# A gated convolution and MLP mix on one core: the work as a graph on a deadline list schedule, exchanges through DRAM in large transfers, a 512-column second DFT step, gate sums on TensorE

## The chip, the cores and the metric

The kernel runs on one core of a Trainium2 chip. The metric is the device time of one launch in microseconds (us), as the median of several executions. Some executions of a kernel are slower as a whole, at a lower granted TensorE clock (the slow state); all times quoted are of runs in the fast state. The engines are called TensorE (PE in profile lines, PEld for its weight loads), VectorE (DVE), ScalarE (ACT), GpSimd (POOL) and SyncE (SP), which issues all DMA transfers here. SBUF is the memory on the chip from which the engines work, PSUM the one that takes the results of matmuls; copying a result from PSUM to SBUF is called its eviction. A slab is one of the 16 groups of 128 positions.

## The reference, cut to what matters

Two branches read the same input `q` of 2048 positions by 640 channels. Branch A is a short shift convolution of `k`, times `v`, then a long convolution along the 2048 positions (by FFT of length 4096), times `q`. Branch B is a mixer and MLP. A sigmoid gate mixes them.

```python
x = A_q
g = sigmoid((x * gate_w).sum(-1, keepdims=True))      # the gate sums
a = _A_ref(x, A_k, A_v, A_shift_k, A_ssm_k, A_ssm_D)  # k shift, kv, rfft * rfft(ssm_k), irfft, q * y
b = _B_ref(x, B_w1, B_w2, B_w3, B_w4)                 # layernorm, w1, gelu, shifts, w2, +x,
                                                      # layernorm, w3 (640->1536), gelu, w4, +
return g * a + (1 - g) * b
```

The FFT is done as matrix products. The 2048 positions lie as 128 partitions by 16. A first step contracts the 128 partitions with DFT tables. Then the 16 residues of each frequency must come to lie in neighbouring partitions: that is the *exchange*. A second step multiplies by small 16-point DFTs, set block by block into a 128x128 matrix. The spectrum of the kernel (H) and of the data (X) are multiplied, and the second step, an exchange and the first step follow backwards (V, inverse).

## The kernel before

The program is written as passes over half of the channels and half of the frequencies, and each engine runs its instructions in program order. The exchange is one transfer from SBUF to SBUF for each of 16 residues, of 80 KB in runs of 640 bytes. W3/W4 come in bursts between passes.

```python
    def exchange(dst, stage, lo):
        nc.sync.dma_start(out=dst, in_=stage.rearrange("(a r) t d -> a r t d", a=8)[:, lo])

    def x_pass(dh, h):
        step1(KV, dh, h, False)                      # first step, into GR (SBUF)
        for kp in range(T1 // 2):
            ps = pst()
            gx = ring.tile([P, 2, DH], BF16, name="gx", bufs=3)
            for j in range(2):
                exchange(gx[:, j, :], GR, 2 * kp + j)
                nc.tensor.matmul(ps[:, j, 0:DH], lhsT=M3[:, 0, :], rhs=gx[:, j, :], start=True, stop=True)
            xs = ring.tile([P, 2, DH], BF16, name="xs")
            nc.scalar.copy(out=xs[:], in_=ps[:, :, 0:DH])
            pq = ring.tile([P, 2, 2, DH], BF16, name="pq", tag="pv", bufs=3)
            nc.vector.tensor_tensor(out=pq[:], in0=xs[:].unsqueeze(2).to_broadcast([P, 2, 2, DH]),
                                    in1=HH[:, 2 * kp:2 * kp + 2], op=ALU.mult)
            pv = pst()
            for j in range(2):
                nc.tensor.matmul(pv[:, j, 0:DH], lhsT=M3[:, 1, :], rhs=pq[:, j, 0, :], start=True, stop=False)
                nc.tensor.matmul(pv[:, j, 0:DH], lhsT=M3[:, 2, :], rhs=pq[:, j, 1, :], start=False, stop=True)
            nc.scalar.copy(out=VR[:, h, 2 * kp:2 * kp + 2, :], in_=pv[:, :, 0:DH])
    ...
    def gate():
        for s in range(T1):
            junk = ring.tile([P, D], BF16, name="junk", tag="xy", bufs=3)
            nc.vector.scalar_tensor_tensor(out=junk[:], in0=QX[:, s, :], scalar=1.0, in1=GW[:], op0=ALU.mult,
                                           op1=ALU.mult, accum_out=Z[:, s:s + 1])
    ...
    x_pass(0, 0)
    h_pass(0, 1)
    w3_chunk(0)
    x_pass(0, 1)
    w4_chunk(0)
    h_pass(1, 0)
    gq_half(0)
    inv(0)
    w3_chunk(1)
    x_pass(1, 0)
    h_pass(1, 1)
    w4_chunk(1)
    w3_chunk(2)
    ...
```

## Time and profile before

| | before |
|---|---|
| time | 528.44 us (528.3 to 528.58, 2 runs) |
| span of the profiled run | 522.9 us |
| TensorE, VectorE, ScalarE busy | 61%, 41%, 30% |
| mean granted TensorE clock | 0.728 |

The page of the profile. The first line below gives the busy time of each engine. The rows under it cut the span in 40 slices: busy tenths, and for PEclk the granted clock in tenths of full speed (9 is 90% or more). The last line is the chain of waits that ended last, by what it spent its time on.

```profile
PE 317.2 (61%) x1597; PEld 159.9 (31%) x1608; DVE 216.5 (41%) x444; ACT 159.0 (30%) x214; POOL 19.7 (4%) x49
...
PE   0196654992146459446945488355488835559797
PEclk9998985896555659755965569556579955558899
DMA  8970206403610250521125510210520241344001
...
DMA gx<-GR 12%; PE ps L451 11%; PE ps L461 10%; DMA vx<-R_70 5%; DVE pq L403 5%; ACT GR L376 4%; PE ps L407 4%; ACT xs L401 4%; DVE bst L220 4%; PE ps L408 3%; SPq L364 3%; DVE R_72 L358 2%; DVE junk L315 2%; DVE R_72 L359 2%; PE ps L302 2%
```

No engine is busy all the time, and the largest entry of the chain is the wait for an exchange. Past the first six slices the clock row follows the busy row: where TensorE is at 5 tenths or less, its clock is mostly 5 or 6.

The timeline of an x pass, VectorE alone (start, duration, what, and in brackets the idle time before and what ended it):

```profile
226.84 0.83 DVE L403 TENSOR_TENSOR pq<-xs,R_71 128x1280 bf16<-128x1280 bf16 x1 [2.63 <-ACT xs L401]
230.30 0.83 DVE L403 TENSOR_TENSOR pq<-xs,R_71 128x1280 bf16<-128x1280 bf16 x1 [2.63 <-ACT xs L401]
233.76 0.82 DVE L403 TENSOR_TENSOR pq<-xs,R_71 128x1280 bf16<-128x1280 bf16 x1 [2.63 <-ACT xs L401]
```

One pair of residues takes 3.46 us, the same each time. In it VectorE works 0.83 us and waits 2.63 us for ScalarE, which waits for TensorE, which has waited for VectorE: the matmuls of the next pair stand behind the products of this one in TensorE's order. TensorE in the same pass, with its wait before the first exchange matmul and then before the products of each pair:

```profile
217.89 0.45 PE L399 MATMUL ps<-gx,M_140 128*128 128x320 bf16 x1 [4.53 <-DMA gx<-GR]
...
224.26 0.42 PE L407 MATMUL ps<-pq,M_140 128*128 128x320 bf16 x1 [1.70 <-DVE pq L403]
...
227.72 0.42 PE L407 MATMUL ps<-pq,M_140 128*128 128x320 bf16 x1 [1.70 <-DVE pq L403]
```

The granted clock was 1.00 up to 214 us, fell to 0.50 from 215 us on, within the wait of 4.53 us, and stayed at 0.50 in the pass (219.5 to 233.5 us), where TensorE is half busy and no gap from 221 us on is longer than 1.70 us.

Busy time of each engine in three stretches (an x pass, an h pass, a W4 burst), with the granted clock. The columns are window, its length, busy us and count of PE, PEld, DVE, ACT, POOL, then clock, DMA share, GB/s:

```profile
142.00:170.00 28.00, 15.16 (x53) 7.21 (x53) 10.31 (x22) 10.27 (x16) 0.45 (x2) 0.50 0.11 24
262.00:283.00 21.00, 8.44 (x25) 1.79 (x24) 0.00 (x0) 9.14 (x15) 0.00 (x0) 0.60 0.41 94
246.24:260.69 14.45, 14.45 (x97) 9.80 (x95) 2.65 (x3) 0.69 (x1) 0.00 (x0) 0.91 0.21 46
```

### The profile page before, as it was taken

To read this page: it belongs to the slowest core of one execution; us is meant where nothing else is said; L and a number is where in the kernel's file an instruction comes from. 1 tells how busy PE (TensorE), PEld (TensorE's weight loads), DVE (VectorE), ACT (ScalarE), POOL (GpSimd) and SP (SyncE) were. 2 spreads that over 40 slices of the span, in tenths; PEclk is the share of its full clock that TensorE was granted. 3 is DMA by queue.
4 is the path that set the end of the run, shared out by engine and by line. 5 is a ranking of instruction groups with operands and counts; after the bars stand their busy time and mean duration, and the time that the engine had idled before them with its cause. 6 is when DMAs were issued, how large, how long until landed. Compare 5 with 4: busy or idle time off the path is not lost.

```text
span 522.9 us, 4484 instructions
## 1 busy us (share of the span) xinstructions
PE 317.2 (61%) x1597; PEld 159.9 (31%) x1608; DVE 216.5 (41%) x444; ACT 159.0 (30%) x214; POOL 19.7 (4%) x49
## 2 busy tenths in 40 slices
PE   0196654992146459446945488355488835559797
PEld 0163320670022124123611143122055312115455
DVE  6988999999841020321201140121014041344402
ACT  0534553005033423533052016335301633100030
POOL 5121000000200000000000000000000000000000
PEclk9998985896555659755965569556579955558899
DMA  8970206403610250521125510210520241344001
GB/s 326 373 269 0 89 14 140 137 8 146 200 42 8 61 128 13 145 52 38 43 59 127 116 26 0 66 36 2 136 64 0 64 104 36 76 101 150 25 1 50
DMA packets 47638, 45.34 MB, mean 87 GB/s; under 512 B 2688, under 2 KB 44545, under 8 KB 47232
## 3 DMA queue, kind: packets, MB, share of 16 engines
q1 hardware_dynamic: 47616, 45.06, 31.0%
q8 instruction: 12, 0.20, 0.2%
q14 instruction: 10, 0.08, 0.0%
HBM read 21.46 MB, written 2.62 MB: 46 GB/s over the span
## 4 chain that ended last, share of the span: by engine, by line
PE 35%; DVE 26%; DMA 18%; ACT 9%; issue 6%; SPq 3%; POOL 1%; ACTq 0%
DMA gx<-GR 12%; PE ps L451 11%; PE ps L461 10%; DMA vx<-R_70 5%; DVE pq L403 5%; ACT GR L376 4%; PE ps L407 4%; ACT xs L401 4%; DVE bst L220 4%; PE ps L408 3%; SPq L364 3%; DVE R_72 L358 2%; DVE junk L315 2%; DVE R_72 L359 2%; PE ps L302 2%
## 5 line engine op out<-in xcount | busy, mean ns | idle before, releaser
L403 DVE TENSOR_TENSOR pq<-xs,R_71 128x1280 bf16<-128x1280 bf16 x32 | 26.4, 824 | 97.2 <-ACT xs L401 97.2
L407 PE MATMUL ps<-pq,M_140 128*128 128x320 bf16 x64 | 28.7, 449 | 56.8 <-DVE pq L403 56.8
L453 ACT ACTIVATE R_78<-ps 128x1024 bf16<-128x1024 f32 x24 | 24.6, 1024 | 120.8 <-PE ps L451 120.8
L451 PE MATMUL ps<-XNT,R_76 128*128 128x512 bf16 x232 | 56.1, 399 | 5.6 <-DVE XNT L247 4.7
L385 PE MATMUL ps<-gx,M_140 128*128 128x320 bf16 x64 | 27.9, 436 | 49.4 <-DMA gx<-GR 48.4
L461 PE MATMUL ps<-R_72,R_78 128*128 128x320 bf16 x384 | 57.7, 314 | 0.0
L464 DVE SCALAR_TENSOR_TENSOR QX<-ps,OMG,QX 128x640 bf16<-128x640 f32 x16 | 14.1, 884 | 81.3 <-PE ps L461 81.3
L376 ACT CAST GR<-ps 128x640 bf16<-128x640 f32 x64 | 39.1, 733 | 20.7 <-PE ps L373 20.7
L461 PEld LDWEIGHTS <-R_78 128*128 128x128 bf16 x384 | 39.3, 102 | 18.6 <-issue 1.0
L409 ACT CAST R_70<-ps 128x640 bf16<-128x640 f32 x32 | 22.1, 692 | 72.1 <-PE ps L408 72.1
L399 PE MATMUL ps<-gx,M_140 128*128 128x320 bf16 x64 | 24.2, 468 | 22.4 <-DMA gx<-GR 22.3
L386 ACT ACTIVATE R_71<-ps 128x640 bf16<-128x640 f32 x32 | 22.5, 704 | 49.4 <-PE ps L385 49.4
L428 PE MATMUL ps<-vx,I_75 128*128 128x320 bf16 x64 | 25.3, 440 | 19.9 <-DMA vx<-R_70 19.4
L451 PEld LDWEIGHTS <-R_76 128*128 128x128 bf16 x240 | 24.5, 103 | 36.2 <-issue 10.1
L431 DVE TENSOR_TENSOR KV<-ps,KV 128x640 bf16<-128x640 f32 x16 | 13.2, 825 | 52.5 <-PE ps L428 52.5
L241 PE MATMUL pt<-IDN,xn 128*128 128x128 bf16 x160 | 15.1, 254 | 29.4 <-DVE xn L236 29.2
L408 PE MATMUL ps<-pq,M_140 128*128 128x320 bf16 x64 | 30.2, 472 | 0.0
L408 PEld LDWEIGHTS <-M_140 128*128 128x128 bf16 x64 | 8.1, 127 | 70.8 <-issue 67.1
L220 DVE BATCH_NORM_STATS2 bst<-QX 128x6 f32<-128x320 bf16 x64 | 27.7, 468 | 4.3 <-DMA QX<-in_A_q_dram 4.3
L264 PE MATMUL ps<-XNT,R_76 128*128 128x512 bf16 x97 | 25.3, 417 | 5.9 <-ACT XNT L245 5.6
L401 ACT CAST xs<-ps 128x640 bf16<-128x640 f32 x32 | 22.3, 696 | 19.5 <-PE ps L399 19.5
L385 PEld LDWEIGHTS <-M_140 128*128 128x128 bf16 x64 | 4.2, 110 | 71.1 <-DMA gx<-GR 71.1
(79 smaller groups left out, 348.9 us busy)
## 6 DMA issues: line engine op xcount, KB each, us to landing
gx<-GR SPq DMA_DIRECT2D x128, 80.0 KB
R_71<-R_71 SPq DMA_DIRECT2D x16, 320.0 KB
vx<-R_70 SPq DMA_DIRECT2D x64, 80.0 KB
R_70<-in_A_k_dram SPq DMA_DIRECT2D x3, 1120.0 KB
QX<-in_A_q_dram SPq DMA_DIRECT2D x4, 640.0 KB
R_71<-in_A_ssm_k_dram SPq DMA_DIRECT2D x5, 512.0 KB
KV<-in_A_v_dram SPq DMA_DIRECT2D x4, 640.0 KB
KV<-in_A_q_dram SPq DMA_DIRECT2D x8, 320.0 KB
```

What stands on the lines that cost most here:

```text
L220: nc.vector.bn_stats(out=st[:, i, j, :], in_=QX[:, s, j * DH:(j + 1) * DH])
L264: nc.tensor.matmul(ps[:, j, :], lhsT=lhsT, rhs=xt[:, k, :], start=(k == 0), stop=(k == DT - 1))
L376: nc.scalar.copy(out=GR[:, 2 * tp:2 * tp + 2, :], in_=ps[:, :, 0:DH])
L385: nc.tensor.matmul(ps[:, j, 0:DH], lhsT=M3[:, 0, :], rhs=gx[:, j, :], start=True, stop=True)
L401: nc.scalar.copy(out=xs[:], in_=ps[:, :, 0:DH])
L403: nc.vector.tensor_tensor(out=pq[:], in0=xs[:].unsqueeze(2).to_broadcast([P, 2, 2, DH]), in1=HH[:, 2 * kp:2 * kp + 2], op=ALU.mult)
L407: nc.tensor.matmul(pv[:, j, 0:DH], lhsT=M3[:, 1, :], rhs=pq[:, j, 0, :], start=True, stop=False)
L408: nc.tensor.matmul(pv[:, j, 0:DH], lhsT=M3[:, 2, :], rhs=pq[:, j, 1, :], start=False, stop=True)
L428: nc.tensor.matmul(ps[:, j, 0:DH], lhsT=I1[:, h, t1, :], rhs=vx[:, j, h, :], start=(h == 0), stop=(h == 1))
L451: nc.tensor.matmul(ps[:, j, :], lhsT=W3[:, k, (f0 + j) * P:(f0 + j + 1) * P], rhs=xt[:, k, :], start=(k == 0), stop=(k == DT - 1))
L453: nc.scalar.activation(out=GTP[:, (3 * c + f0 // 4) % 5, f0 % 4:f0 % 4 + 2, :], in_=ps[:], func=ACT.Gelu_apprx_tanh)
L461: nc.tensor.matmul(ps[:, j, 0:DH], lhsT=GTP[:, (3 * c + f // 4) % 5, f % 4, i * P:(i + 1) * P], rhs=W4[:, f, j * DH:(j + 1) * DH], start=( ...
```

## The change

The intent is to let W3/W4 and the transforms run at the same time, to make exchanges few and large, and to take work off VectorE. Every piece of work becomes a node with a cost on each engine that could do it, dependences, buffers of small rings, and a deadline. A greedy list scheduler, run while the program is built, puts the nodes into one static order for each engine. The text below is cut to the core.

```diff
+class Plan:
+    def add(self, name, alts, fn, deps=(), bufs=(), mode=None, tgt=None, after=0.0, nbytes=0, rate=370.0):
+    ...
+    def schedule(self):            # rank = latest start, from deadlines and successors; greedy by rank
+    ...
-    def exchange(dst, stage, lo):
-        nc.sync.dma_start(out=dst, in_=stage.rearrange("(a r) t d -> a r t d", a=8)[:, lo])
+            wr.append(pl.dma("%sw%d" % (pref, c), lambda e, c=c, sb=sb: nc.sync.dma_start(
+                out=dram.rearrange("h p t d -> p h t d")[:, :, 2 * c:2 * c + 2, :], in_=SG[:, sb.idx]), ...
+    ...
+        def rd(dram, e, xb, h=h, hb=hb):
+            nc.sync.dma_start(out=XIN[:, xb.idx].rearrange("p (m d) -> p m d", m=8),
+                              in_=dram[h].rearrange("p t d -> (p t) d").rearrange("(m q) d -> q m d", q=P)[:, hb:hb + 8, :])
+    ...
-                nc.tensor.matmul(ps[:, j, 0:DH], lhsT=M3[:, 0, :], rhs=gx[:, j, :], start=True, stop=True)
+            for C in range(2):     # the other branch, TILE64, works in 64x64 quarters; it is off
+                nc.tensor.matmul(pt[:, C, :], lhsT=M3[:, m, :], rhs=rhs_fn(None, C), start=start, stop=stop)
+    ...
-            nc.vector.scalar_tensor_tensor(out=junk[:], in0=QX[:, s, :], scalar=1.0, in1=GW[:], op0=ALU.mult,
-                                           op1=ALU.mult, accum_out=Z[:, s:s + 1])
+                        for k in range(DT):
+                            nc.tensor.matmul(ps(pb)[:, 1, i:i + 1], lhsT=XNT[:, xb.idx, k, i * P:(i + 1) * P],
+                                             rhs=GWT[:, k:k + 1], start=(k == 0), stop=(k == DT - 1))
+    ...
+    plan = pl.schedule()
+    with tc.manual_schedule():
+        for n in plan:
+            n.fn(n.eng)
```

The gate sums on TensorE use the normalized rows that are there already for W1, and are turned back into sums of `q` with mean and deviation. The graph also shares evictions between ScalarE and VectorE, takes the statistics of the second layernorm from accumulators, and fuses gate, `q` and eviction in the output stage.

## The prediction

> **What bounds the kernel now.** No engine does. The summary of the profile has TensorE at 61% (317.2 us), VectorE 41% (216.5), ScalarE 30%. The chain of waits is a serial alternation: "DMA gx<-GR" 12%, "DMA vx<-R_70" 5%, its issue on SP 3%, pq 5%, xs 4%, GR eviction 4%. The timeline of an x pass repeats every 3.46 us: ScalarE copy 0.70, VectorE product 0.83, four matmuls, eviction, next pair; TensorE has about 1.5 us of work in it. The stretches of transform passes (75-92, 142-195, 208-246, 262-306, 320-381, 413-475 us: some 230 us) hold TensorE about half busy, and the granted clock there is 0.50-0.60, against 0.9-1.0 in the W3/W4 bursts. That agrees with the Trainium skill, "TensorE: Matmul & The Clock Gate" (Part 1: idle windows put the array at half clock). So serial exchange costs twice: the wait and the slow clock.
>
> **What the change does.** Matmul columns stay the same (about 528 thousand): W1-W4, 132 first-step and 64 inverse matmuls as before; the second step becomes 160 matmuls of 512 columns in place of 256 of 320. In dense bursts the trace shows 0.20-0.24 us per 512 columns (one W3 chunk: 60 in 13.9 us) and 0.135-0.155 per 320 (W4: 96 in 13.0-15.0). 500 x 0.23 + 676 x 0.145 + 272 transposes x 0.07 + gate matmuls 5 = 237 us of TensorE if warm.
> VectorE, by issue spacing (0.73 us for 640 PSUM elements or 1280 bf16): removed are 12 us of gate sums and half of the layernorm statistics; added are half of the evictions (28 of 1024 elements, about 1.13 us; 22 of 640). Sum about 220-225 us. ScalarE stays near 150.
> DMA: 192 exchange issues of 80 KB at 0.6 us each on SP become about 36 large ones, but through DRAM: about 36 MB of exchange and swaps instead of 21, about 60 MB in all; at the 345-370 GB/s of the first load stretch about 170 us, now mostly hidden.
>
> **How much is on the critical path.** Nearly all of the exchange waits, since the list schedule puts W3/W4 work between transform matmuls. What remains serial: all first-step outputs must be written before a read, and all four V writes before the inverse. Stages, estimated from those durations:
> - load, layernorm, W1, H step 1, W2: three engines each about 75-80 us, coupled through four PSUM buffers: about 97;
> - k shift (64 products, 47 us of VectorE) with X step 1 and W3/W4: about 60;
> - second step and products (VectorE about 62): about 75;
> - V write, reads, inverse, 16 fused outputs (VectorE 18 us, DMA 10 MB), stores: about 35;
> - outside the span (528.4 against 522.9): 5.5.
> About 272; with static-order stalls I predict 280 us, 80% range 256 to 322. Faster by over 2%: 0.985; within 2%: 0.01; slower: 0.005.
>
> **What would show each step right.** TensorE over 80% busy, mean clock 0.85-0.95 instead of 0.73; VectorE 75-85% and the co-limit; no exchange in the chain above 5% except around the X read and in the last 35 us; DMA share 60-70%, few packets under 1 KB. The gate sums should vanish from the 62-73 us chain.
>
> **What would make it wrong.** A static order that misjudges DMA latency: one late landing stalls all engines and drops the clock. DRAM turnarounds above 5 us, or 1280-byte rows well under 300 GB/s, would push it towards 320. VectorE evictions slower than estimated add directly in the last three stages. If stages overlap better than assumed, 255.

## The result, and the profile after

| | before | after |
|---|---|---|
| time | 528.44 us | 280.64 us (280.39 to 280.9, 2 runs) |
| ratio of fast runs | 1 | 0.531, 95% interval 0.5295 to 0.5325 |
| span of the profiled run | 522.9 us | 278.6 us |
| TensorE, VectorE, ScalarE busy | 61%, 41%, 30% | 87%, 83%, 52% |
| mean granted clock | 0.728 | 0.983 |

Ratios here and below are the mean time of one kernel's fast runs over that of the other's fast runs of the same rounds, so not quite the ratio of the medians that stand beside them. The experiments ran later, on several chips, each beside the kernel before but not beside the kernel after; the median of the kernel before lay between 526.66 and 529.52 us there. Differences of a few us from the kernel after are therefore good to some 2 us only (an estimate from the intervals of the ratios).

The same lines of the page, after:

```profile
PE 243.2 (87%) x1597; PEld 144.7 (52%) x1597; DVE 230.7 (83%) x424; ACT 144.9 (52%) x177; POOL 26.5 (10%) x59
...
PE   4389989699999999989979899999999799899650
PEclk9999999889999999999999999999999999999995
DMA  7998414029994021294041999852999450589974
...
PE PS L763 13%; PE PS L860 11%; PE PS L775 11%; DMA CJ<-in_A_q_dram 5%; DMA RK<-GHD 4%; PE PS L580 4%; DVE RK L823 4%; DVE RK L827 4%; PE PS L677 3%; DMA RK<-in_A_k_dram 3%; PE PS L731 2%; DVE SX L348 2%; DVE RK L957 2%; DVE W L426 2%; DVE QX L781 1%
```

Between the load phase and the tail TensorE stands at 8 or 9 in nearly all slices, with the clock at 8 or 9 from the first slice to the 39th. The chain is now 47% matmuls and 31% VectorE, and the one exchange at the top of it is 4%. The work itself has hardly changed. That both pages count 1597 matmuls is chance: in the first trace 11 matmul records are missing (it has 1608 weight loads), and the second kernel has 160 matmuls of 512 columns in the second step in place of 256 of 320, and 85 of one column for the gate (1608 - 96 + 85 = 1597). The smaller busy time comes mostly from the second step: with the same number of columns it is 111.0 us busy before and 40.7 after, while W4 is 57.7 and 54.4. The clock is a part of that; how large a part, no run separates.

Five stretches after (same columns): the load phase; W1, the first step of H and part of W2; the rest of W2 and the k shift with the first step of X; the second step; and the tail.

```profile
0.00:24.00 24.00, 14.30 (x111) 12.20 (x112) 19.96 (x44) 11.55 (x11) 9.64 (x32) 1.00 0.92 320
24.00:78.00 54.00, 49.07 (x381) 29.34 (x380) 46.96 (x152) 43.44 (x60) 8.27 (x18) 0.97 0.54 200
78.00:153.00 75.00, 71.72 (x463) 43.62 (x463) 72.92 (x125) 37.02 (x56) 8.58 (x11) 1.00 0.37 130
165.00:225.00 60.00, 57.91 (x326) 30.14 (x325) 49.91 (x49) 37.51 (x38) 0.00 (x0) 1.00 0.78 271
250.00:278.60 28.60, 15.96 (x108) 10.12 (x105) 21.67 (x35) 0.00 (x0) 0.00 (x0) 0.89 0.83 282
```

What is left over lies at the ends. In the first 24 us TensorE works 14.3 us beside loads at about 320 GB/s. In the last 28.6 us it works 16.0, and the chain of the tail tells why:

```profile
250.27 1.74 DVE RK L957 x3
252.01 6.86 DMA CJ<-in_A_q_dram
258.89 1.68 DVE RK L957 x2
...
263.11 4.07 DMA CJ<-in_A_q_dram
...
268.97 3.68 DMA CJ<-in_A_q_dram
```

`CJ<-in_A_q` is the reload of `q` for the output stage: it has two buffers, so a load can start only when a product has given one back, and the chain waits 6.86 + 4.07 + 3.68 = 14.6 us for three of them.

### The profile page after: what moved, and what is told of

Read it like the earlier page. It is cut to its first block, busy times and chain, and to the rows that moved or that the text cites. A ratio compares the mean times of both kernels' runs of the same rounds, so it can differ in the third digit from the quotient of the medians.

```text
span 278.6 us, 4239 instructions
## 1 busy us (share of the span) xinstructions
PE 243.2 (87%) x1597; PEld 144.7 (52%) x1597; DVE 230.7 (83%) x424; ACT 144.9 (52%) x177; POOL 26.5 (10%) x59
## 2 busy tenths in 40 slices
DMA packets 32788, 60.89 MB, mean 219 GB/s; under 512 B 2304, under 2 KB 19457, under 8 KB 32384
## 4 chain that ended last, share of the span: by engine, by line
PE 47%; DVE 31%; DMA 12%; issue 4%; ACT 4%; POOL 0%; SPq 0%; DVEq 0%; ACTq 0%; POOLq 0%
PE PS L763 13%; PE PS L860 11%; PE PS L775 11%; DMA CJ<-in_A_q_dram 5%; DMA RK<-GHD 4%; PE PS L580 4%; DVE RK L823 4%; DVE RK L827 4%; PE PS L677 3%; DMA RK<-in_A_k_dram 3%; PE PS L731 2%; DVE SX L348 2%; DVE RK L957 2%; DVE W L426 2%; DVE QX L781 1%
## 5 line engine op out<-in xcount | busy, mean ns | idle before, releaser
L775 PE MATMUL PS<-W,RG 128*128 128x320 bf16 x384 | 54.4, 299 | 2.9 <-ACT RG L767 1.4
L763 PE MATMUL PS<-XNT,W 128*128 128x512 bf16 x240 | 54.4, 379 | 0.1
L344 ACT CAST SX<-PS 128x640 bf16<-128x640 f32 (+1 forms) x55 | 40.2, 775 | 26.9 <-PE PS L731 22.7
L775 PEld LDWEIGHTS <-RG 128*128 128x128 bf16 x384 | 37.5, 98 | 19.3 <-issue 4.2
L767 ACT ACTIVATE RG<-PS 128x1024 bf16<-128x1024 f32 x24 | 24.6, 1023 | 25.8 <-PE PS L763 25.6
L763 PEld LDWEIGHTS <-W 128*128 128x128 bf16 x240 | 23.5, 98 | 27.8 <-issue 0.7
L348 DVE CAST SX<-PS 128x640 bf16<-128x640 f32 (+1 forms) x29 | 26.1, 914 | 4.4 <-issue 3.3
L781 DVE SCALAR_TENSOR_TENSOR QX<-PS,ZG,QX 128x640 bf16<-128x640 f32 x16 | 14.1, 881 | 17.9 <-PE PS L775 17.9
L677 PE MATMUL PS<-R 128*128 128x320 bf16 x160 | 25.0, 307 | 0.5 <-DVE ZG L606 0.3
L916 DVE TENSOR_TENSOR SX<-SX,R 128x2048 bf16<-128x2048 bf16 x20 | 24.1, 1219 | 0.2
L677 PEld LDWEIGHTS <-R 128*128 128x128 bf16 x160 | 16.0, 101 | 8.1 <-issue 1.3
L580 PEld LDWEIGHTS <-R 128*128 128x128 bf16 x100 | 9.9, 99 | 11.7 <-issue 0.6
```

What stands on the lines that cost most here:

```text
L344: nc.scalar.copy(out=o, in_=i)
L348: nc.vector.tensor_copy(out=o, in_=i)
L580: nc.tensor.matmul(ps(pb)[:, j, :], lhsT=lhsT, rhs=XNT[:, xb.idx, k, :], start=(k == 0), stop=(k == DT - 1))
L677: nc.tensor.matmul(ps(pb)[:, j, 0:DH], lhsT=gst_ap(k, s), rhs=W2[:, k, j * DH:(j + 1) * DH], start=(k == 0), stop=(k == DT - 1))
L763: nc.tensor.matmul(ps(pb)[:, j, :], lhsT=W3[:, k, (f0 + j) * P:(f0 + j + 1) * P], rhs=XNT[:, xb.idx, k, :], start=(k == 0), stop=(k == DT ...
L767: gns.append(pl.add("g2.%d.%d" % (c, f0), {A: act_p(1024)}, lambda e, f0=f0, pb=pb, gb=gb: nc.scalar.activation(out=GTP[:, gb.idx, f0 % 4: ...
```

## The experiments

The theory from the prediction was that the exchange cost before was a chain of waits, paid a second time in the clock, and that filling the waits with W3/W4 is what removes it. Rivals: the DRAM exchange in large transfers does it alone; or any order that keeps engines busy does.

### W3/W4 back in bursts

The list schedule stays, but W3 and W4 of one chunk form a block of their own on TensorE between the transform blocks.

```diff
+    bl_t = [xpe, <second step, chunks 0 and 1>, <chunks 2 and 3>, ivpe]
+    for i in range(4):
+        for p in bl_t[i]:
+            p.deps.extend(w4all[i])
+        if i < 3:
+            for p in w3all[i + 1]:
+                p.deps.extend(bl_t[i])
     plan = pl.schedule()
```

> The kernel after, with W3/W4 kept out of the transform work: four bursts (W3 and W4 of one chunk), each a block of its own on TensorE between first-step X, second-step halves and inverse, as the kernel before had them. Exchange through DRAM, big packets, 512-column second step and gate sums stay. Theory (overlap of W3/W4 with transforms is the largest part of the gain): 315 to 345 us, TensorE below 80% busy, the transform blocks limited by VectorE. Rival (the new exchange did it, the order is secondary): 280 to 290 us.

Measured: 321.36 us, ratio to before 0.6108 (0.6077 to 0.6139), TensorE 79% busy, clock 0.912. That is within what the theory expected, and the rival that only the exchange matters falls. But seen from before, the larger part of the gain is still there without any W3/W4 between transform matmuls. So a second theory was needed: within a transform block, the list schedule also keeps several tiles in flight.

### The same, and the second step one tile at a time

```diff
             pe = pl.add("x2.%d.%d" % (cc, u), {PE: PE2}, ...,
-                        [ldx, m3n], [pb, xb, sb], mode=md, tgt=TG["x2"](cc, u))
+                        [ldx, m3n] + lastpv[-1:], [pb, xb, sb], mode=md, tgt=TG["x2"](cc, u))
```

> The burst run plus one more constraint: each second-step X tile waits until the products of the tile before it are through TensorE, which is the order of the x pass in the kernel before (copy, product, matmuls, next tile). Exchange through DRAM stays. Theory (the list schedule also gained by keeping several tiles in flight, about 4.4 us a tile in series against some 2.7 in the burst run, 20 tiles): 345 to 365 us. Rival (VectorE holds the second step anyway): 320 to 328 us.

Measured: 387.06 us, ratio 0.7341 (0.7283 to 0.7399), clock 0.838; one of four runs was slow (392.92 us) and is left out of both. More than expected. The timeline of VectorE in this run shows the alternation of the kernel before again:

```profile
204.75 1.23 DVE L348 CAST SX<-PS 128x1024 bf16<-128x1024 f32 x1 [2.84 <-PE PS L863]
206.01 1.22 DVE L921 TENSOR_TENSOR SX<-SX,R 128x2048 bf16<-128x2048 bf16 x1
210.07 1.23 DVE L348 CAST SX<-PS 128x1024 bf16<-128x1024 f32 x1 [2.84 <-PE PS L863]
```

A tile takes 5.32 us (204.75 to 210.07) and not the 4.4 that I expected. In the stretch from 180 to 235 us TensorE is 25.4 us busy at a granted clock of 0.69, so the slow clock came back with the waits. In the burst run four products take 4.93 us:

```profile
198.68 4.93 DVE L921 TENSOR_TENSOR SX<-SX,R 128x2048 bf16<-128x2048 bf16 x4
```

The 20 products stand in two groups of ten. From the first start to the last, a group takes 44.4 and 44.9 us in this run and about 15.9 and 14.1 us in the burst run. That is 59 us of the difference of 66 us (387.06 less 321.36), so it is the tiles in series, and not something else in the new plan, that cost nearly all of it. Several tiles in flight are worth some 66 us here, more than the interleaving of W3/W4.

### The kernel before with W3/W4 in pieces

W3 and W4 become generators that give out one unit after each pair step of a pass; the exchange and the tiles stay as they were.

```diff
     def x_pass(dh, h, fill=None):
...
+            take(fill)
             pv = pst()
...
+    fill = work()                    # w3_chunk(c), w4_chunk(c) for each c, 40 units of matmuls
-    x_pass(0, 0)
-    h_pass(0, 1)
-    w3_chunk(0)
+    x_pass(0, 0, fill)
+    h_pass(0, 1, fill)
```

> The kernel before, with its old exchange (192 small SBUF to SBUF transfers) and old tiles, but W3/W4 given out in 40 pieces between the pair steps of the x, h and inverse passes instead of seven bursts of 123 us in all. Theory (overlap is the largest part): 400 to 430 us, the bursts gone and the clock in the passes near 0.9. Rival (the old exchange limits whatever the order): above 470 us.

Measured: 441.31 us, ratio 0.8372 (0.8334 to 0.841). A little slower than the range of the theory, far from the rival. The order alone is worth 85 us in the old exchange (the edit also moves the 16 final sums and stores behind the last pass). The clock row suggests why it was not more: the fill runs out.

```profile
PE 288.7 (66%) x1597; PEld 155.9 (36%) x1608; DVE 215.5 (49%) x444; ACT 157.1 (36%) x214; POOL 19.5 (4%) x49
...
PE   0077788359922799589499679979595645255451
PEclk9999888659975699699699969999697655655555
```

The last W4 matmul starts at 331.6 us of the 439.1. In the last nine slices, from 340 us on, TensorE is at 1 to 6 tenths and the clock at 5 or 6, as in the passes before the change.

### The kernel before, kept warm

Matmuls whose results are overwritten by the real ones keep TensorE busy while it waits. They take no wait away.

```diff
             pv = pst()
+            warm(pv, 8)              # 8 matmuls of 320 columns into the tile, then the real ones
             for j in range(2):
```

with 4 to 6 of them before each exchange pair in the h, x and inverse passes.

> The kernel before, plus dummy matmuls of 320 columns into tiles that the real matmuls then overwrite (8 before each product pair, 4 to 6 before each exchange pair), so that TensorE stays busy in the transform passes. No wait is removed. Theory (the half clock costs a part by itself): the clock in the x passes goes from 0.59 to about 1.0, the 3.46 us period to about 2.7, total 495 to 510 us. Rival (only the waits matter): 520 to 535 us, or slower by the dummies.

Measured: 474.17 us, ratio 0.9001 (0.8966 to 0.9036), correct result, mean clock 0.941 in place of 0.728. This is a larger effect than I expected, although 672 matmuls were added. The x pass before and with the dummies, same window of the two runs (the columns as above):

```profile
142.00:170.00 28.00, 24.63 (x152) 15.62 (x152) 12.32 (x30) 15.35 (x24) 0.45 (x2) 0.88 0.15 34
```

The clock there is 0.88 where it was 0.50 (the last 7 us of the window already belong to the next pass in this run). The first and the last product of the x pass after it:

```profile
208.62 0.82 DVE L411 TENSOR_TENSOR pq<-xs,R 128x1280 bf16<-128x1280 bf16 x1 [2.00 <-ACT xs L409]
...
226.83 0.83 DVE L411 TENSOR_TENSOR pq<-xs,R 128x1280 bf16<-128x1280 bf16 x1 [2.12 <-ACT xs L409]
```

The eight products start 2.60 us apart on average, instead of 3.46. So about 52 us of the kernel before were the slow clock by itself, and rather more, since the 672 dummies take time of TensorE too. The waits for exchanges are still there; part of them is now SyncE's issuing, 8% of the chain (`SPq L364`) where it was 3%. The Trainium skill, "TensorE: Matmul & The Clock Gate", Part 1, says that a window of idleness puts the array at half clock until it has been busy again. The x pass before agrees with it: the clock fell in the wait of 4.53 us and did not come back while TensorE was half busy, with gaps of 1.70 us. Here, with the gaps filled, it did.

### Priority by place in the program

```diff
+        for n in nodes:
+            n.rank = float(n.seq) * 1000.0
         engs = ("PE", "ACT", "DVE", "POOL", "SP")
```

> The kernel after with the same greedy list scheduling, but each node's priority is its place in the program (W3/W4 stand before the k shift and the X transform there) in place of the deadlines. Theory (deadlines matter: the long chain k shift, X transform, products, inverse must start first): 310 to 350 us, a tail with TensorE half idle. Rival (any work-conserving order does): 280 to 290 us.

Measured: 337.41 us, ratio 0.6406 (0.6374 to 0.6438), TensorE 76% busy. The theory holds: with this priority W3/W4 is done as soon as it can be, its last matmul starts at 218.4 us of 335.3, and none is left for the transforms behind it.

```profile
PE   0288799989989997999799999993279575615480
PEclk9999789999999999999999999998569979785957
```

From the 28th slice on TensorE is below 8 tenths in all slices but two. Deadlines are worth some 57 us of the 248 against this order.

### Exchange in half rows, and in pieces of 80 KB

Both keep the order of the kernel after. The first cuts each exchange into runs of 640 bytes (120 transfers in place of 36), the second into 80 KB pieces as well (384 transfers).

```diff
+    def cut_m(outs, ins):
+        for j in range(2):
+            js = slice(j * DH, (j + 1) * DH)
+            if HALF:
+                nc.sync.dma_start(out=outs[:, :, js], in_=ins[:, :, js])
+                continue
+            for m in range(8):
+                nc.sync.dma_start(out=outs[:, m, js], in_=ins[:, m, js])
```

> The kernel after with every exchange transfer cut so that each contiguous run is half a row (640 bytes, as in the kernel before) in place of 1280 to 2560; 36 exchange transfers become 120. From the two profiles (DMA share over packets: about 0.055 us per packet of mean 946 bytes before, 0.084 of 1850 after) the exchange's DMA time grows from about 91 to 135 us of the 16 engines. Theory (mostly hidden): 284 to 295 us. Rival (large packets are what made the exchange cheap): above 305 us.

Measured: 284.34 us, ratio 0.5387 (0.535 to 0.5423), just under 4 us slower than after by the medians. The packets went from 32788 to 64853, and the queue's share from 62.0% of 278.6 us to 66.9% of 283.0, so 173 to 189 us; I had worked out 44 us more and it was 17.

> As the half-row run, but each transfer is also cut to pieces of 80 KB, as in the kernel before: 384 exchange transfers. At 0.6 us of issue each that is 230 us of SP, and the V reads before the inverse become 64 issues (38 us in place of the 15 us that the data takes). Theory (the number of issues, not the run length, is what the large transfers save): 315 to 350 us. Rival (run length): within 5 us of the half-row run.

Measured: 329.08 us, ratio 0.6222 (0.6186 to 0.6258). With nearly the same number of packets (69080), 264 more transfers cost 45 us more. One issue takes 0.43 us of SyncE in the middle here (0.59 in the kernel before). The chain of this run names SyncE:

```profile
PE PS L796 14%; SPq L738 11%; PE PS L893 6%; PE PS L678 5%; SPq L750 4%; DMA CJ<-in_A_q_dram 3%; PE PS L581 3%; PE PS L808 3%; DVE SX L349 3%; DMA RK<-in_A_k_dram 2%; PE PS L765 2%; DVE RK L856 2%; DMA RK<-GHD 2%; DVE W L427 2%; DVE RK L860 2%
```

`SPq L738` is the issue of reads and V writes, 11% of the span. So what makes large transfers cheap here is that they are few, not that their runs are long. The Trainium skill, "DMA: Bandwidth & Descriptors", "Rules for kernel authors", advises to coalesce small transfers into one large one; this run agrees, and still at 80 KB a piece, above the 64 KB that the page names: 329.08 us with 384 transfers, 284.34 with 120.

### Gate sums on VectorE, replanned, and with the order kept

The 16 products with accumulation return, the one-column matmuls go. In the first run the list scheduler planned anew.

```diff
-                            nc.tensor.matmul(ps(pb)[:, 1, i:i + 1], ...)
+    zn = [pl.add("zs%d" % s, {V: dve(D)}, lambda e, s=s: nc.vector.scalar_tensor_tensor(
+        out=GJ, in0=QX[:, s, :], scalar=1.0, in1=GW, op0=ALU.mult, op1=ALU.mult,
+        accum_out=ZG[:, 0, s:s + 1]), [ldgw, ldq[s // 2]], tgt=40000.0) for s in range(T1)]
```

> The kernel after with the gate sums back on VectorE (16 products with accumulation, 0.73 to 0.82 us each, replanned by the same list schedule), the 85 one-column matmuls and the copies of their sums taken out. Theory (VectorE is in the chain of the first 78 us): 286 to 293 us. Rival (hidden behind TensorE): 279 to 282 us.

Measured: 304.88 us, ratio 0.5777 (0.5751 to 0.5804): much slower than either theory. The timeline of TensorE in this run:

```profile
119.59 3.42 PE L760 MATMUL PS<-W,RG 128*128 128x320 bf16 x24 [0.78 <-ACT SX L344]
144.78 0.69 PE L716 MATMUL PS<-KV,F 128*128 128x320 bf16 x2 [21.77 <-DVE QX L766]
```

TensorE stands for 21.8 us. The wait ends with the W4 eviction on VectorE (`QX L766`), which needs the gate. The few tiny gate instructions had come behind the whole k shift in VectorE's new order, at 142 us; until then the W4 results sat in PSUM tiles and no tile was free. That is the plan, not the sums. So the second run keeps the order of the kernel after and only puts the 16 products in between.

```diff
             n.fn(n.eng)
+            # (stands for several lines) from slab 7's statistics on: after a layernorm or shift instruction on VectorE, one product
+            nc.vector.scalar_tensor_tensor(out=GJ, in0=QX[:, g, :], scalar=1.0, in1=GW, op0=ALU.mult, op1=ALU.mult,
+                                           accum_out=ZG[:, 0, g:g + 1])
```

> Gate sums on VectorE again, but with the planned order of the kernel after kept instruction for instruction: the 16 products (0.75 us each, 12 us) are only put in between the layernorm and shift instructions from 25 us on, and the 85 one-column matmuls leave TensorE. Theory (the replanned gate run lost 24 us mainly because its gate came at 142 us and TensorE stood 21.8 us behind full PSUM tiles; the direct cost is the 12 us of VectorE in a chain that VectorE holds): 286 to 294 us. Rival A (the sums themselves cost all of it): above 300 us. Rival B (hidden): 279 to 283 us.

Measured: 288.88 us, ratio 0.5472 (0.5445 to 0.5499), within the theory's range. Sums on TensorE are worth about 8 us: less than the 12 us of VectorE work, so part of that seems to have been hidden. The other 16 us of the first run were its order.

### Five q buffers

```diff
-    r_qr = Ring("qr", 2)
+    r_qr = Ring("qr", 5)           # three more in the first-step DFT table, free by then
```

> The kernel after with five buffers in place of two for the reloaded q of the output stage (three of them in the DFT table, free by then), so that the loads need not wait for the products. In the profile after, the chain has 14.6 us of waits for these loads after 252 us. Theory: 266 to 273 us. Rival (VectorE, 21.7 us busy of the last 28.6, or the V reads limit the tail anyway): 276 to 281 us.

Measured: 275.33 us, ratio 0.5209 (0.5184 to 0.5233). Faster, but by 5 us (1.9%) and not by 8 to 14, just outside both expected ranges. The chain, which the profile follows back only to 252.9 us in this run, holds no wait for a load:

```profile
254.41 0.87 DVE RK L962
255.28 0.40 DVE QX L967
...
258.14 1.54 DVE RK L962 x2
259.68 0.80 DVE QX L967 x2
...
261.31 1.67 DVE RK L962 x2
262.97 0.81 DVE QX L967 x2
```

`DVE RK` is the fused product (0.8 us a slab), `DVE QX` the addition (0.4). VectorE goes from one to the next almost without a gap: it was the limit right behind the loads, as the rival had it in part. Before that TensorE is full: 14.96 us busy in the 15 from 245 to 260 us.

### The second step in quarters of the array

The kernel has this form as a switch: four 64x64 matmuls for each tile half.

```diff
-    TILE64 = False
+    TILE64 = True
```

> The kernel after with its own other form of the second step: four 64x64 quarter-array matmuls of 512 columns per tile in place of two full 128x128 ones (640 against 160 in the second step loads and products... four per half as many columns each). Theory (TensorE is 87% busy and bounds the stretch from 24 to 250 us, quarters run side by side): 12 to 17 us of TensorE saved, 264 to 272 us. Rival (quarters do not overlap well, or the second step is held by VectorE there): 279 to 300 us.

Measured: 277.18 us, ratio 0.5244 (0.5214 to 0.5274), 1.2% under the kernel after, and between the two expected ranges. The quarters do run side by side. The timelines of TensorE, first quarters, then full matmuls of the kernel after:

```profile
176.16 0.63 PE L856 MATMUL PS<-SX,M 64*64 64x512 bf16 x8 [0.25 <-DVE SX L916]
176.59 0.63 PE L856 MATMUL PS<-RK,M 64*64 64x512 bf16 x8
```

```profile
178.59 1.93 PE L860 MATMUL PS<-SX,M 128*128 128x512 bf16 x8
180.36 1.17 PE L860 MATMUL PS<-RK,M 128*128 128x512 bf16 x4
```

The eight quarter matmuls at 176.16, one product tile, take 0.43 us until the next group at 176.59. The eight full ones at 178.59 are two product tiles and take 1.77 us until the next group, so 0.88 us for one tile. The Trainium skill, "TensorE: Matmul & The Clock Gate", Part 3, says that tiles of the array run at the same time, and this agrees. (The run has 320 quarter matmuls for 160 full ones, not the 640 of the expectation.) TensorE's busy time fell from 243.2 to 231.5 us, and from 57.9 to 52.7 us of the 60 between 165 and 225 us. The chain of this run waits from 153.4 to 172.0 us for the last X write and the first X read, and has evictions on ScalarE and VectorE between the matmuls behind it; that this is what kept the gain at 3.5 us is read from the chain, not tested. The clock is another candidate, also untested: from 186 to 188 us, among quarter matmuls, it was 0.50, although no gap of TensorE from 181 us on had been longer than 0.52 us, and over the 60 us it was 0.97 in place of 1.00.

### The three together, and the tail's eviction on ScalarE

```diff
+    TILE64 = True, five q buffers, and in the output stage:
-                nc.vector.scalar_tensor_tensor(out=GY..., in0=ps(pb)..., scalar=G32[:, s:s + 1], in1=QR..., ...)
+                nc.scalar.activation(out=GY..., in_=ps(pb)..., func=ACT.Copy, scale=G32[:, s:s + 1])
+                nc.vector.tensor_tensor(out=GY[:, yb.idx], in0=GY[:, yb.idx], in1=QR(qb.idx)[:, s % 2, :], op=ALU.mult)
```

> A version meant to beat both kernels, three changes to the kernel after together: five q buffers (the run with them alone gained 5 us), the quarter-array second step (alone it gained 3.5 us, with 17 us less TensorE work), and in the output stage ScalarE, idle there, takes the scaled copy out of PSUM so that VectorE has 0.8 us per slab in place of 1.2 to 1.3. Theory (the tail is held by VectorE, and by TensorE before it): 262 to 269 us. Rival (what is left is the exchange's write-to-read turnaround and the evictions): 270 to 274 us.

Measured: 267.65 us (266.01 to 269.01), ratio 0.5068 (0.5039 to 0.5098), correct. This is the fastest version, 4.6% under the kernel after by the medians, and within the theory's range. The three changes were not run in pairs, so what ScalarE's share gives is not separated: the other two gained 5.3 and 3.5 us alone, all three 13.0.

## Why the prediction was right

**The time.** 280 us was forecast and 280.64 measured. Part of that is luck. The front was close: the last W2 matmul ended at 97.6 us (estimate 97) and the last X write was issued at 156.7 (157). The second step took 80.5 us, to its last matmul at 237.2, and not 75. The tail took 41 us, not 35; the two q buffers explain much of it (five gained 5.3). The time outside the span was 2.0 us (280.64 less 278.6), not 5.5: that estimate set the median of two runs against the span of another run, which must have been faster, since in all later runs of the kernel before time and span differ by about 2.1 us. These errors add up to about 8 us, and 8 us is what I had added for stalls, without a stage to put them in.

**What bounds the kernel before.** Right, and now measured: the serial exchange cost twice. The slow clock alone is 52 us or more (the warm run). No single engine was the limit, since order alone took 85 us off.

**"Nearly all of the exchange waits, since the list schedule puts W3/W4 work between transform matmuls".** The size was right, the reason was incomplete. On the way from before to after, the runs are:

| step | us |
|---|---|
| before | 528 |
| exchange through DRAM, tiles of 1024, new front; W3/W4 in bursts, one second-step tile at a time | 387 |
| several second-step tiles in flight | 321 |
| W3/W4 between the transforms | 281 |

So 141, 66 and 41 us. W3/W4 between transforms is the smallest of the three, and what I named as the cause. The middle step, which the prediction did not separate, is larger; 59 us of it are seen in the trace, tile by tile. The first step holds the large transfers (cutting them to 80 KB costs 48 us), the gate sums (8 us) and things that no run took apart, such as the fuller front. These sizes depend on where one starts: with the old exchange, W3/W4 in pieces gained 85. Each of these kernels was also planned anew, and the gate run shows that a new plan can by itself lose some 16 us, so the steps are sizes, not exact shares.

**Work on each engine.** TensorE 237 us forecast, 243.2 busy; VectorE 220 to 225, 230.7 busy; DMA 170 us, 62.0% of 278.6 = 173. TensorE over 80% (87%), VectorE 75 to 85% (83%), DMA 60 to 70% (62%) all came as said. The clock came out better than the 0.85 to 0.95 that I expected: 0.983.

**What would have made it wrong.** The fear of a static order that stalls everything was sound: the kernel after escaped it, the replanned gate run did not. The fear of DRAM turnarounds above 5 us came true without the harm: reads of 1280 KB took 7.2 and 8.0 us (medians) from issue to landing, and the first read of X was issued 10.8 us after the last write of X (167.5 and 156.7 us), but TensorE was 10.4 us busy of the 12 between 153 and 165 us and 57.9 of the next 60. The fear of slow 1280-byte rows was not sound: DMA moved 350 GB/s in those 12 us, and even half rows cost only 4 us.

What stays open is how much of the first step is due to the DRAM route itself. A run with the old SBUF to SBUF transfers inside the new graph was not made. Nor was the simplest rival tried: the kernel before with nothing changed but the next pair's matmuls put ahead of this pair's products.

## What to carry to other kernels

When the engines take turns and TensorE's clock is low, look first for a loop in which each engine waits for the one before it, and put the next tile's matmuls ahead of this tile's products (66 us here, inside the new graph); then put independent matmuls into what waits remain (41 us here), and see the clock rise with them. A list schedule over a graph does both, but its deadlines carry the result: check after each replanning that tiny instructions that many others wait for, here the gate, have not slid behind a long block. Few large transfers matter because each issue holds the issuing engine (0.43 us here). When TensorE is full in the middle, look at the ends: work on the tail and the quarters together gained 13 us here; the first 24 us were not tried.

## What the Trainium skill lacked or had wrong

- "TensorE: Matmul & The Clock Gate" names loop order and padding as remedies for the clock falling between waits. It does not name dummy matmuls into tiles that are overwritten anyway; here they took the clock from 0.728 to 0.941 and the time from 526.66 to 474.17 us, with every wait left in place.
- "DMA: Bandwidth & Descriptors", section "Issuing engines are not separate DMA queues", calls the time to start a DMA usually small relative to the DMA itself. At 80 KB a piece it was not: 0.59 us an issue in the kernel before, where the data took an estimated 0.44 us (128 packets of 640 bytes at 0.055 us each, from that trace, over 16 engines); and with 384 pieces instead of 120, at the same run length, the kernel after took 329.08 us in place of 284.34.
- "TensorE: Matmul & The Clock Gate", Part 3, measures packed tiles of 32 rows, 32 columns or both, but no 64x64 quarters, and "TensorEngine Tiling (Array Packing)" lists them with a theoretical speedup only: eight of 512 columns here take 0.43 us, where the same work as four full, zero-blocked matmuls took 0.88 us.
- No page has anything on static list schedules: a plan that put a handful of 0.17 us gate instructions behind the k shift, at 142 us, left TensorE idle for 21.8 us through full PSUM tiles.
